# Moving the row-norm scaling between GpSimd and VectorE in an attention and mixer kernel on Trainium2: squares, scales and transposes of the second and third batch reordered

## The chip, the cores and the metric

The kernel runs on one core of one Trainium2 chip. The metric is the device time of one execution in microseconds. Five engines work side by side: TensorE (PE in the profile) for matmuls, VectorE (DVE), ScalarE (ACT), GpSimd (POOL) and SyncE (SP), which here only issues transfers.

## The reference

Cosine attention over 8 batches of 12 heads, 448 rows and head size 64, and a channel mixer behind it:

```python
q_n = q / (np.linalg.norm(q, axis=-1, keepdims=True) + 1e-06)
k_n = k / (np.linalg.norm(k, axis=-1, keepdims=True) + 1e-06)
scores = np.matmul(q_n, k_n.transpose(0, 1, 3, 2)) / tau
scores = scores - np.max(scores, axis=-1, keepdims=True)
attn = np.exp(scores)
attn = attn / (np.sum(attn, axis=-1, keepdims=True) + 1e-09)
out = np.matmul(attn, v)
...
x = np.ascontiguousarray(attn_out.transpose(0, 2, 1, 3)).reshape(B, S, H * D)
...
xt = x.transpose(0, 2, 1)
h = xt @ U @ V
u = x + h.transpose(0, 2, 1)
ch = np.maximum(u @ w_ch1, 0.0) @ w_ch2
return (u + ch).astype(np.float32)
```

x is 8 x 448 x 768, U is 448 x 32, w_ch1 is 768 x 3072, w_ch2 is 3072 x 768. Everything is given and returned in float32.

## The kernel before

**Tiling.** The 12 heads of a batch are 6 pairs, and the 48 pairs are numbered through: pair 6 is the first of the second batch (b = 1), pair 12 the first of the third. A row of 448 positions is cut into four chunks of up to 128. Loading and preparation go by groups of pairs: groups 0 to 3 are the first batch (of 1, 1, 2 and 2 pairs), and from then on every group has two pairs: group 4 is pairs 6 and 7, group 5 pairs 8 and 9, group 6 pairs 10 and 11, group 7 pairs 12 and 13, group 8 pairs 14 and 15. The loads of q, k and v go to three sets of buffers in turn (`qst`, `kst`, `vst`), the scaled q and k to two (`qk`).

**Preparation of a group** (class `Prep`). `square` (L234) multiplies q or k by itself on GpSimd; `reduce` (L239, VectorE) sums the squares of a row; `root` (L244, L245, ScalarE) takes the square root as Ln and Exp; `invert` (L251, L253, VectorE) makes the inverse; `scale` (L259, on the engine that is given) multiplies q or k of one pair by it and writes bf16. `values` (L267, GpSimd) casts v.

**A pair.** T transposes scaled q and k, into `qkT`: below pair 12 as eight PE matmuls (L288) with an eviction by VectorE (L293), from pair 12 on as one DMA transpose that SP issues (L303). Sc makes the scores (`sc`, L312 and L318) and ScalarE their exponentials (`E`, L326 and L329). V is the product with v in two halves (`av` or `up`, L349 and L356), and VectorE divides by the row sums into X (L367, L368). A (L389) and the following transpose of X (L403) and H (L414) add the low-rank part; VectorE or ScalarE then evicts into `uE` or `uO` (L419). `A` of a pair reads X of both its halves. From pair 12 on variants with DMA transposes (XT, A2, H2) do the same.

**The mixer of a batch** is cut in pieces that are handed out among the pairs of the next batch (the list `fill`; `f(n)` takes the next n). `steps_m1` has 24 pieces, six matmuls each into `mp` (L483), with a relu on ScalarE (L487) or VectorE (L489), whichever a running estimate finds free first (`est.act_first`). `steps_m2` has 24 (first batch) or 32 pieces of six matmuls (L510); after four of them a block of 128 x 384 is complete, goes to `o_sb` (L524, L526, L528), and SP stores it in two halves (`t4`, L534; `t3` or `t4e`, L537 and L540). In the first batch three matmuls with the identity (L520) add u.

**Order.** Every engine runs its instructions in the order in which the program names them; nothing is rescheduled. The first six pairs follow a list written by hand (`ORDER`), at whose end stand the scales of pair 6, `sc6q.v sc6k.v`, both on VectorE. Then a loop goes over pairs 6 to 48: for each pair an `order` of steps, between which `spread` gives out pieces of the mixer by weight. `put(n, i, ...)` hangs a step of preparation behind step i of pair n. SP's queue holds the loads, the DMA transposes and the stores, all in program order; GpSimd's own queue holds the loads of the mixer's weights (`load_w1`, `load_w2`).

Before the change the squares of a group are one step (k, then q), GpSimd scales k and VectorE q, and a line in front of the loop reads:

```python
    preps[4].values()
    preps[4].scale(1, 1, P_)
    preps[4].scale(0, 1, V_)
    fill.extend(steps_m1(0) + steps_m2(0))
    f(3)
    T(NP)
    f(1)
```

Here NP is 6, `V_` is VectorE and `P_` is GpSimd; scale's first argument is 0 for q and 1 for k, the second the pair in the group.

Of the kernel before, what the change touches and what calls it, by code (L numbers as in the profile page):

```python
# [22 lines left out]
def kernel(  # L23
# [16 lines left out]
    nc = tc.nc  # L40

    B, H, S, D = q.shape
# [3 lines left out]
    NP = H // 2  # L46
# [37 lines left out]
    est = Estimate()  # L84
# [85 lines left out]
    groups = []  # L170
# [101 lines left out]
    def by_dma(n):  # L272

        return n >= 2 * NP
# [57 lines left out]
    def step_S(b, p, cs):  # L332
        for c in cs:
            pe_S(b, p, c)
            exp_S(b, p, c)
# [47 lines left out]
    def u_of(b):  # L383
        return uE if b % 2 == 0 else uO
# [83 lines left out]
    def turn(b, half):  # L468
# [4 lines left out]
            out=t.rearrange("p k c d -> p (k c) d"),  # L473
            in_=u_of(b)[:, 3 * half:3 * half + 3, :].rearrange("p k s -> p (k s)"))

    def steps_m1(b):
        u = u_of(b)
        o = 64 if b % 2 == 0 else 0

        def one(f):  # L480
            mp = psum.tile([128, S], FP, name="mp", tag="ps_m", bufs=2)
            for cc in range(CC):
                nc.tensor.matmul(out=mp, lhsT=w1_sb[:, cc, f * 128:(f + 1) * 128],  # L483
                                 rhs=u[:, cc, 0:S], start=(cc == 0), stop=(cc == CC - 1))
            est.pe(1.13)
            if est.act_first(0.55, 0.62):
                nc.scalar.activation(out=relu[:, f, o:o + S], in_=mp, func=AF.Relu)  # L487
            else:
                nc.vector.tensor_scalar_max(out=relu[:, f, o:o + S], in0=mp, scalar1=0.0)  # L489
            if b > 0 and f in (3, 12):  # L490
                turn(b, f // 12)

        return [lambda f=f: one(f) for f in range(NC)]

    def steps_m2(b):
        u = u_of(b)
        if b % 2 == 0:
            chunks = [(64 + 128 * c, 128 * c, c) for c in range(3)]
        else:
            chunks = [(384, 384, 3)] + [(128 * c, 128 * c, c) for c in range(3)]  # L500
        steps = []
        state = {}

        def part(half, ci, lo, hi):
            r0, u0, c = chunks[ci]
            if lo == 0:
                state["mp"] = psum.tile([128, HC], FP, name="mp", tag="ps_m", bufs=2)
            mp = state["mp"]
            for f in range(lo, hi):
                nc.tensor.matmul(out=mp, lhsT=relu[:, f, r0:r0 + 128],  # L510
                                 rhs=w2_sb[:, f, half * HC:(half + 1) * HC],
                                 start=(f == 0), stop=(b > 0 and f == NC - 1), skip_group_check=True)
            est.pe(0.97)
            if hi < NC:
                return
            o = work.tile([128, HC], FP, name="o_sb", tag="o_sb", bufs=3)
            if b == 0:
                for i in range(3):
                    cc = half * 3 + i
                    nc.tensor.matmul(out=mp[:, i * 128:(i + 1) * 128], lhsT=u[:, cc, u0:u0 + 128],  # L520
                                     rhs=ident, start=False, stop=(i == 2), skip_group_check=True)
                est.pe(0.17)
                if est.act_first(0.48, 0.55):
                    nc.scalar.copy(out=o, in_=mp)  # L524
                else:
                    nc.vector.tensor_copy(out=o, in_=mp)  # L526
            else:
                nc.vector.tensor_add(o.rearrange("p (k d) -> p k d", d=128),  # L528
                                     mp.rearrange("p (k d) -> p k d", d=128),
                                     ut_of[(b, half)][:, :, c, :])  # L530
                est.dve(0.55)
            cols = slice(half * HC, (half + 1) * HC)
            t4 = out[b, 0:256, cols].rearrange("(p c) d -> c p d", c=4)
            nc.sync.dma_start(out=t4[c], in_=o[0:64, :])  # L534
            if c < 3:
                t3 = out[b, 256:448, cols].rearrange("(p c) d -> c p d", c=3)
                nc.sync.dma_start(out=t3[c], in_=o[64:128, :])  # L537
            else:
                t4e = out[b - 1, 0:256, cols].rearrange("(p c) d -> c p d", c=4)
                nc.sync.dma_start(out=t4e[3], in_=o[64:128, :])  # L540

        for half in range(2):
            for ci in range(len(chunks)):
                for i in range(4):
                    steps.append(lambda half=half, ci=ci, i=i: part(half, ci, 6 * i, 6 * i + 6))
        return steps
# [4 lines left out]
    fill = []  # L551
    preps = [Prep(gi) for gi in range(len(groups))]
    first_pair = [b * NP + p0 for b, p0, _ in groups]

    def f(n):
        for _ in range(n):
            fill.pop(0)()
# [16 lines left out]
    V_, P_ = nc.vector, nc.gpsimd  # L574

    def T(n):
        step_T(*pairs[n])

    def Sc(n, *cs):
        step_S(*pairs[n], cs)  # L580

    def V(n, half):
        step_V(*pairs[n], half)

    def A(n):
        step_A(*pairs[n])

    def Hs(n):
        step_H(*pairs[n])
# [77 lines left out]
    load_w2(0, 0, 12)  # L667
    load_w2(0, 12, 24)
    preps[4].values()
    preps[4].scale(1, 1, P_)  # L670
    preps[4].scale(0, 1, V_)
    fill.extend(steps_m1(0) + steps_m2(0))
    f(3)
    T(NP)
    f(1)


# [2 lines left out]
    def put(n, at, fn):  # L680
        after.setdefault((n, at), []).append(fn)

    for gi in range(5, len(groups)):
        m, n, g = first_pair[gi], groups[gi][2], preps[gi]
        two = range(n)
        if m - 3 < NP:
            at = [(NP, 0), (NP, 6), (NP, 5), (NP, 6), (NP + 1, 0), (NP + 1, 1), (NP + 1, 2), (NP + 1, 3)]
        elif m == 2 * NP:
            at = [(m - 2, i) for i in (0, 6, 3, 4, 5)] + [(m - 1, i) for i in (0, 1, 2)]
        elif m - 3 == NP + 1:  # L690
            at = [(NP + 1, 6), (NP + 2, 5)] + [(NP + 2, i) for i in (3, 4, 5, 6)] + [(NP + 3, 0), (NP + 3, 2)]
        else:
            at = [(m - 3, 0), (m - 3, 5)] + [(m - 2, i) for i in range(6)]
        put(*at[0], lambda g=g: (g.square(1), g.square(0)))
        put(*at[1], lambda g=g: g.values())
        put(*at[2], lambda g=g: g.reduce(1))
        put(*at[3], lambda g=g: g.reduce(0))
        put(*at[4], lambda g=g: g.root())
        put(*at[5], lambda g=g: (g.invert(), [g.scale(1, j, P_) for j in two]))
        for j in two:  # L700
            put(*at[6 + j], lambda g=g, j=j: g.scale(0, j, V_))
        if gi > 5 and m - 6 <= NP:
            put(*((NP, 3), (NP + 3, 0))[gi - 6], lambda gi=gi: load_all(gi))
        elif gi > 5:
            put(m - 6, 4, lambda gi=gi: load(gi, "q", nc.sync))
            put(m - 5, 5, lambda gi=gi: load(gi, "k", nc.sync))
            put(m - 4, 3, lambda gi=gi: load(gi, "v", nc.sync))
        if by_dma(m):
            put(m - 1, -1 if m > 2 * NP else 2, lambda m=m: T(m))
            put(m - 1, 0 if m > 2 * NP else 4, lambda m=m: T(m + 1))  # L710
# [21 lines left out]
    for n in range(NP, NPAIR + 1):  # L732
        b, p = pairs[n] if n < NPAIR else (B, 0)
# [2 lines left out]
        late = n > FIRST2  # L736
        for g in after.pop((n, -1), []):
            g()
        if not late:
            if n % 2 == 0:  # L740

                order = [
                    (1, lambda: Sc(n, 0, 1)),
                    (0, done and (lambda: V(n - 1, 0))),
                    (1, not by_dma(n + 1) and (lambda: T(n + 1))),
                    (0, lambda: Sc(n, 3)),
                    (1, done and (lambda: V(n - 1, 1))),
                    (0, done and (lambda: A(n - 1))),
                    (1, lambda: (Sc(n, 2), Sc(n + 1, 0))),
                    (1, done and (lambda: Hs(n - 1))),  # L750
                ]
            else:
                order = [
                    (1, lambda: Sc(n, 1, 2)),
                    (1, lambda: V(n - 1, 0)),
                    (0, lambda: Sc(n, 3)),
                    (1, not by_dma(n + 1) and (lambda: T(n + 1))),
                    (1, lambda: V(n - 1, 1)),
                    (1, lambda: A(n - 1)),
                    (0, lambda: Hs(n - 1)),  # L760
                ]
            last = p == 0 and done
            nf = len(fill) if last else 5
            spread(n, order, nf)
            if last:
                f(len(fill))
                fill.extend(steps_m1(b - 1) + steps_m2(b - 1))
            continue
# [80 lines left out]
```

## Time and profile before

| what | value |
|---|---|
| time, median of 3 runs | 596.05 us (595.59 to 596.13) |
| profiled run | 595.31 us, span in the trace 593.5 us |
| PE busy | 574.4 us (97%) |
| VectorE busy | 258.7 us (44%) |
| ScalarE busy | 263.6 us (44%) |
| GpSimd busy | 190.1 us (32%) |
| granted PE clock, mean | 0.995 |
| HBM read, written | 52.19 MB, 11.01 MB |

A profile is one execution. Its span starts with the first instruction; times in the text count from there. A line of a group or of the timeline names the engine, the line of the kernel, the operation, and the tile that is written and those that are read (out<-in); the idle time in brackets is what the engine stood before it, with the instruction that ended the wait. An idle engine costs time only where the work that ends last runs through it. The span is some 2 us shorter than the time of the same run.

### The profile page before, as it was taken

The page shows a single profiled execution, that of the slowest core. Times are in us where ns is not written, and L with a number is a line of the kernel's source. Part 1 is how long each engine was busy: PE and PEld are TensorE (multiplying, and loading weights), DVE is VectorE, ACT ScalarE, POOL GpSimd, SP SyncE. Part 2 cuts the span into 40 slices and gives each one's busy share as a digit, 9 for nine tenths or more (in the row PEclk, how much of TensorE's full clock was granted, in tenths as well). Part 3 has the DMA queues.
Part 4 walks back from the last instruction along what each step waited for, and adds up shares of the span by engine and source line. Part 5 has one row for each costly group of instructions (what it writes and reads, how often), then busy time and mean ns, then how long its engine had stood idle before and what let it go on. Part 6 is the DMA issues. An engine that isn't in the chain of part 4 may idle for free.

```text
span 593.5 us, 11562 instructions
## 1 busy us (share of the span) xinstructions
PE 574.4 (97%) x4729; PEld 327.7 (55%) x4729; DVE 258.7 (44%) x499; ACT 263.6 (44%) x452; POOL 190.1 (32%) x161
## 2 busy tenths in 40 slices
PE   6988997999999999999999999999999999999996
PEld 5654564554555555655555555555556545555564
DVE  6875665516345255633354263643355242220011
ACT  5965453446434465246343465345542465314300
POOL 8674555504054053143152251351340410000000
PEclk9999998999999999999999999999999999999999
DMA  6999999463474763673655753863646631222012
GB/s 165 204 230 233 241 240 196 112 117 82 112 152 114 155 134 93 141 170 85 127 135 112 160 129 86 159 158 76 140 110 138 134 64 28 51 64 47 6 48 54
DMA packets 138581, 74.20 MB, mean 125 GB/s; under 512 B 85568, under 2 KB 138352, under 8 KB 138528
## 3 DMA queue, kind: packets, MB, share of 16 engines
q1 hardware_dynamic: 128496, 63.06, 46.9%
q0 software_dynamic: 9728, 10.18, 10.1%
q8 instruction: 37, 0.61, 0.4%
q10 hardware_dynamic: 304, 0.21, 0.1%
q14 instruction: 16, 0.13, 0.1%
HBM read 52.19 MB, written 11.01 MB: 106 GB/s over the span
## 4 chain that ended last, share of the span: by engine, by line
PE 90%; DVE 3%; DMA 3%; SPq 1%; ACT 1%; POOL 1%; issue 1%; POOLq 0%; DVEq 0%; ACTq 0%
PE mp L510 37%; PE mp L483 35%; PE sc L318 5%; PE av L356 3%; DMA kst<-in_k_dram 2%; PE up L356 2%; PE sc L312 1%; DVE qk L259 1%; PE av L349 1%; PE up L349 1%; PE up L442 1%; PE tp L288 1%; DMA qst<-in_q_dram 1%; POOL sq L234 1%; PE av L455 1%
## 5 line engine op out<-in xcount | busy, mean ns | idle before, releaser
L510 PE MATMUL mp<-w_sb,relu 128*128 128x384 bf16 x1344 | 237.2, 328 | 0.0
L510 PEld LDWEIGHTS <-relu 128*128 128x128 bf16 x1344 | 126.0, 98 | 92.4 <-issue 15.8
L483 PEld LDWEIGHTS <-w_sb 128*128 128x128 bf16 x1152 | 107.3, 98 | 101.1 <-issue 10.2
L329 ACT ACTIVATE E<-sc 128x896 bf16<-128x896 f32 x144 | 124.5, 916 | 67.2 <-PE sc L318 66.6
L487 ACT ACTIVATE relu<-mp 128x448 bf16<-128x448 f32 x166 | 90.3, 544 | 138.0 <-PE mp L483 137.9
L259 POOL TENSOR_TENSOR qk<-kst,inv 128x512 bf16<-128x512 f32 x44 | 53.0, 1223 | 264.0 <-DVE inv L253 257.0
L483 PE MATMUL mp<-uE,w_sb 128*128 128x448 bf16 x576 | 119.3, 353 | 0.8 <-DVE relu L489 0.8
L483 PE MATMUL mp<-uO,w_sb 128*128 128x448 bf16 x576 | 115.6, 353 | 0.0
L528 DVE TENSOR_TENSOR o_sb<-mp,ut 128x384 f32<-128x384 f32 x50 | 27.8, 556 | 122.6 <-PE mp L510 122.6
L239 DVE TENSOR_REDUCE ss<-sq 128x16 f32<-128x1024 f32 (+1 forms) x50 | 56.8, 1165 | 4.1 <-POOL sq L234 2.9
L259 DVE TENSOR_TENSOR qk<-qst,inv 128x512 bf16<-128x512 f32 x44 | 51.7, 1183 | 0.6 <-DVE inv L253 0.2
L367 DVE RECIPROCAL rd<-av 128x4 f32<-128x4 f32 x54 | 9.7, 179 | 91.8 <-PE av L356 91.8
L234 POOL TENSOR_TENSOR sq<-kst 128x1024 f32<-128x1024 f32 (+1 forms) x23 | 44.4, 1932 | 14.6 <-DMA kst<-in_k_dram 14.6
L356 PEld LDWEIGHTS <-E 128*128 128x128 bf16 x1152 | 45.0, 97 | 0.0
L234 POOL TENSOR_TENSOR sq<-qst 128x1024 f32<-128x1024 f32 x21 | 43.3, 2061 | 0.0
L318 PE MATMUL sc<-qkT 64*128 64x448 bf16 x288 | 41.3, 355 | 0.9 <-ACT E L326 0.3
L326 ACT ACTIVATE E<-sc 128x448 bf16<-128x448 f32 x48 | 25.9, 540 | 32.4 <-PE sc L312 32.4
L267 POOL CAST v<-vst 128x1024 bf16<-128x1024 f32 (+1 forms) x25 | 28.4, 1138 | 9.5 <-DMA vst<-in_v_dram 6.9
L356 PE MATMUL av<-v,E 128*128 128x65 bf16 x648 | 29.1, 193 | 0.0
L489 DVE TENSOR_SCALAR relu<-mp 128x448 bf16<-128x448 f32 x26 | 16.0, 620 | 29.7 <-PE mp L483 29.3
L349 PEld LDWEIGHTS <-E 128*128 128x128 bf16 x192 | 17.9, 98 | 16.2 <-DVE uO L460 0.8
L367 DVE RECIPROCAL rd<-up 128x4 f32<-128x4 f32 x36 | 6.5, 181 | 44.9 <-PE up L356 44.9
(93 smaller groups left out, 321.9 us busy)
## 6 DMA issues: line engine op xcount, KB each, us to landing
out_dram<-o_sb SPq DMA_DIRECT2D x112, 96.0 KB, 2.2
w_sb<-in_moe_w_ch_dram POOLq DMA_DIRECT2D x8, 1152.0 KB, 25.8
qst<-in_q_dram SPq DMA_DIRECT2D x23, 256.0 KB, 4.0
vst<-in_v_dram SPq DMA_DIRECT2D x46, 128.0 KB, 2.8
kst<-in_k_dram SPq DMA_DIRECT2D x44, 128.0 KB, 2.7
qst<-in_q_dram SPq DMA_DIRECT2D x23, 192.0 KB, 4.0
vst<-in_v_dram SPq DMA_DIRECT2D x46, 96.0 KB, 2.6
kst<-in_k_dram SPq DMA_DIRECT2D x44, 96.0 KB, 2.7
```

Source lines behind the costliest of these rows:

```text
L234: nc.gpsimd.tensor_mul(sq[:, 0:self.nh * 4, :], self.flat(t), self.flat(t))
L239: nc.vector.reduce_sum(self.ss[:, j, 0:self.nh * 4], self.sq[j][:, 0:self.nh * 4, :], axis=AX.X)
L259: eng.tensor_mul(qks[self.gi % 2][:, j, i, :, :, :], t[:, 2 * j:2 * j + 2, :, :].rearrange("p h c d -> p c h d"), iv.unsqueeze(3).to_broad ...
L267: nc.gpsimd.tensor_copy(out=self.flat(v65[self.s])[:, :, 0:D], in_=self.flat(vst[self.s]))
L318: nc.tensor.matmul(out=sc[:, h, 0:S], lhsT=t[r, 1, c * 128:(c + 1) * 128], rhs=t[r, 0, 0:S], start=True, stop=True)
L329: nc.scalar.activation(out=e[:, 2 * c:2 * c + 2, 0:S], in_=sc[:, :, 0:S], func=AF.Exp)
L349: nc.tensor.matmul(out=av[:, i, :, :], lhsT=e[:, 6, ic * 128:(ic + 1) * 128], rhs=vv[:, 2 * j:2 * j + 2, 3, :], start=(i == 0), stop=False ...
L356: nc.tensor.matmul(out=av[:, i, h, :], lhsT=e[:, 2 * c + h, ic * 128:(ic + 1) * 128], rhs=vv[:, 2 * j + h, c, :], start=False, stop=(i == ...
L483: nc.tensor.matmul(out=mp, lhsT=w1_sb[:, cc, f * 128:(f + 1) * 128], rhs=u[:, cc, 0:S], start=(cc == 0), stop=(cc == CC - 1))
L487: nc.scalar.activation(out=relu[:, f, o:o + S], in_=mp, func=AF.Relu)
L510: nc.tensor.matmul(out=mp, lhsT=relu[:, f, r0:r0 + 128], rhs=w2_sb[:, f, half * HC:(half + 1) * HC], start=(f == 0), stop=(b > 0 and f == ...
L528: nc.vector.tensor_add(o.rearrange("p (k d) -> p k d", d=128), mp.rearrange("p (k d) -> p k d", d=128), ut_of[(b, half)][:, :, c, :])
```

## The change

It does four things. In preparation, q and k of a group are squared in steps of their own, with places of their own, and so are the scales: for group 5 (pairs 8 and 9) VectorE scales both k and q; for group 7 (pairs 12 and 13) GpSimd scales both; the other groups keep k on GpSimd and q on VectorE, and k of pair 7 moves to VectorE. Where a group's sums are taken, the order of q and k may turn: in group 6 VectorE now sums q before k. The transpose of pair 6 comes after five pieces of the mixer and not three, and before the scales of pair 7; the transposes of pairs 8 and 10 come after the second half of V of the pair before. During pair 7 all relus go to ScalarE (`busy`). And for the second half of the columns of the last batch three stores (`t3`) are issued by ScalarE and not by SP. In even pairs a transpose that is left to DMA now counts in the weights of `spread`, which moves mixer pieces in pair 12.

```diff
+    state_of = {"busy": False}
...
-            if est.act_first(0.55, 0.62):
+            if state_of["busy"] or est.act_first(0.55, 0.62):
...
-                nc.sync.dma_start(out=t3[c], in_=o[64:128, :])
+                other = nc.scalar if b == B - 1 and half == 1 else nc.sync
+                other.dma_start(out=t3[c], in_=o[64:128, :])
...
-    preps[4].scale(1, 1, P_)
+    fill.extend(steps_m1(0) + steps_m2(0))
+    f(5)
+    T(NP)
     preps[4].scale(0, 1, V_)
-    fill.extend(steps_m1(0) + steps_m2(0))
-    f(3)
-    T(NP)
+    preps[4].scale(1, 1, V_)
     f(1)
...
+        scales = [(1, 0, P_), (1, 1, P_), (0, 0, V_), (0, 1, V_)]
+        if m == NP + 2:
+            at = [(NP, 0), (NP, 1), (NP + 1, 6), (NP, 5), (NP + 1, 0), (NP + 1, 1)]
+            when = [(NP + 1, 2), (NP + 1, 5), (NP + 1, 2), (NP + 1, 5)]
+            scales = [(1, 0, V_), (1, 1, V_), (0, 0, V_), (0, 1, V_)]
+        elif m == NP + 4:
+            at = [(NP + 2, 0), (NP + 2, 0), (NP + 2, 6), (NP + 2, 3), (NP + 2, 4), (NP + 2, 5)]
+            when = [(NP + 2, 6), (NP + 2, 6), (NP + 3, 0), (NP + 3, 2)]
         elif m == 2 * NP:
-            at = [(m - 2, i) for i in (0, 6, 3, 4, 5)] + [(m - 1, i) for i in (0, 1, 2)]
+            at = [(m - 2, 0), (m - 2, 0), (m - 2, 6), (m - 2, 4), (m - 2, 3), (m - 2, 5)]
+            when = [(m - 1, 0)] * 4
+            scales = [(1, 0, P_), (0, 0, P_), (1, 1, P_), (0, 1, P_)]
         else:
-            at = [(m - 3, 0), (m - 3, 5)] + [(m - 2, i) for i in range(6)]
+            d = 1 if m == 2 * NP + 2 else 0
+            at = [(m - 3, 0), (m - 3, 0), (m - 3, 5)] + [(m - 2, i + d) for i in (1, 0, 2)]
+            when = [(m - 2, i + d) for i in (3, 3, 4, 5)]
+        put(*at[1], lambda g=g: g.square(1))
+        put(*at[0], lambda g=g: g.square(0))
+        put(*at[2], lambda g=g: g.values())
+        put(*at[4], lambda g=g: g.reduce(1))
         put(*at[3], lambda g=g: g.reduce(0))
+        put(*at[5], lambda g=g: g.root())
+        put(*when[0], lambda g=g: g.invert())
+        for x, w in zip(scales, when):
+            put(*w, lambda g=g, x=x: g.scale(*x))
...
+        state_of["busy"] = n == NP + 1
...
-                    (1, not by_dma(n + 1) and (lambda: T(n + 1))),
+                    (1, None if by_dma(n + 1) else (lambda: T(n + 1))),
...
+                    (1, lambda: V(n - 1, 1)),
                     (1, not by_dma(n + 1) and (lambda: T(n + 1))),
-                    (1, lambda: V(n - 1, 1)),
```

## The prediction

> **What bounds the kernel now.** I read the busy time by stage first, then who TensorE (PE) waited for, then the timelines around each wait. By stage (columns: window, its length, busy us and instruction count of PE, weight loads, VectorE, ScalarE, GpSimd, then granted PE clock, DMA share, GB/s):
>
> ```profile
> 39.30:62.00 22.70, 18.40 (x125) 9.09 (x124) 14.24 (x22) 11.27 (x20) 13.46 (x11) 1.00 1.16 235
> 62.00:85.00 23.00, 23.00 (x220) 13.35 (x219) 12.96 (x25) 13.52 (x25) 12.95 (x11) 1.00 1.23 240
> 85.00:99.00 14.00, 11.69 (x128) 7.47 (x125) 10.54 (x15) 6.06 (x11) 6.85 (x6) 1.00 1.16 227
> 99.00:124.00 25.00, 23.73 (x175) 13.94 (x175) 8.95 (x17) 8.22 (x15) 9.82 (x9) 0.93 0.43 104
> 124.00:560.00 436.00, 435.92 (x3452) 242.08 (x3450) 177.29 (x340) 195.90 (x337) 116.66 (x77) 1.00 0.50 111
> ```
>
> From 124 to 560 us PE is busy 435.92 of 436.00: it sets the time there, and nothing but fewer PE instructions could shorten it. What can be won lies before 124 us: idle PE and one stretch at a clock of 0.93. PE's waits in 40 to 125 us (us in total, times, longest):
>
> ```profile
> PE av L389 <- DVE X L368: 3.0, 1, 3.0
> PE tp L288 <- DVE qk L259: 1.8, 2, 1.7
> PE tp L288 <- POOL qk L259: 1.4, 1, 1.4
> PE mp L483 <- DVE relu L489: 0.8, 1, 0.8
> PE av L349 <- DVE X L368: 0.5, 1, 0.5
> PE sc L318 <- ACT E L326: 0.3, 1, 0.3
> ```
>
> The largest, in the timeline of PE, then of VectorE, then of GpSimd (start, length, operation, idle before):
>
> ```profile
> 99.72 0.48 PE L389 MATMUL av<-X,U_sb 128*128 128x128 bf16 x4 [3.04 <-DVE X L368]
> 100.38 3.54 PE L510 MATMUL mp<-w_sb,relu 128*128 128x384 bf16 x12
> 94.48 4.63 DVE L259 TENSOR_TENSOR qk<-qst,inv 128x512 bf16<-128x512 f32 x2
> 99.24 0.42 DVE L368 TENSOR_TENSOR X<-av,rd 128x256 bf16<-128x256 f32 x1
> 94.37 1.89 POOL L234 TENSOR_TENSOR sq<-kst 128x1024 f32<-128x1024 f32 x1
> 96.22 2.34 POOL L234 TENSOR_TENSOR sq<-qst 128x1024 f32<-128x1024 f32 x1
> ```
>
> The two q scales of pairs 12 and 13 take 4.63 us where the shortest row of that kind takes 0.68, because GpSimd squares the next group meanwhile. X of pair 10 stands behind them, and A of pair 10 waits 3.04. Then twelve m2 matmuls take 3.54 us instead of 2.06 to 2.12: the clock record shows 0.5 from 99.87 for 3.41 us.
>
> **What the skill says.** The Trainium skill, "GPSIMD Engine Reference", section 1 (Specifications): GpSimd's SBUF interface is shared with VectorE, in contention with VectorE instructions that have two SBUF inputs. The trace agrees: 0.68 alone, 1.3 to 1.5 beside GpSimd's scales, 2.3 beside its squares. "TensorE: Matmul & The Clock Gate", Part 1: the clock falls to half after an idle window of about 3.4 us and returns after a busy one. Here 3.04 us of idling did it, 1.66 did not. "DMA: Bandwidth & Descriptors", "Queues, rings and completion order": an engine's descriptors are consumed in ring order; SP's transfers landed in issue order up to 100 us here.
>
> **The change, part by part.** PE's order is the same from the end of pair 12 to the end of the kernel, so only 40 to 122 us and the last store can change. A modelled matmul end lies 0.16 after the next start, so idle of x costs x + 0.16. One m1 part (six L483 matmuls) is 1.13 us, one m2 part 0.97.
>
> 1. T(6) after five m1 parts, not three. VectorE's first two scales end at about 43.7 with GpSimd idle (44.56 before); PE comes at 39.30 + 5 x 1.13 + 0.09 = 45.07. The 1.66 idle (1.82 lost) goes.
>
> 2. Both scales of pair 7 move to VectorE behind T(6)'s eviction (46.35) while GpSimd squares q, landed at 46.11, until 48.16. One scale contended (to 48.3), one alone: 49.0. T(7) would be ready at 48.28: new wait 0.75 (0 without contention, 1.3 with both contended).
>
> 3. With two relus moved, the wait of m1 for VectorE (0.78, 0.94 lost) goes; a relu now stands before exp on ScalarE: Sc(7,0) waits 0.24 more.
>
> 4. Pair 8's scales are all on VectorE with GpSimd idle (its next input lands at 65.2): four of 0.68. T(8), moved behind V(6,1), waits 0.25 instead of 1.38 and 0.15. Sc(8) thus starts at about 64.3 with two m1 parts more done, against 65.62.
>
> 5. Here the gain shrinks. k of pairs 10 and 11 lands at 65.20 as before, since SP's order is unchanged up to there. GpSimd squares k, then q:
>
> ```profile
> 65.36 1.89 POOL L234 TENSOR_TENSOR sq<-kst 128x1024 f32<-128x1024 f32 x1 [3.72 <-DMA kst<-in_k_dram]
> 67.21 1.89 POOL L234 TENSOR_TENSOR sq<-qst 128x1024 f32<-128x1024 f32 x1
> ```
>
> VectorE now reduces q first: it stands at 69.15 until the later square, reduces until 70.28, and only then makes X(7,1), at 70.9. A(7), ready at 69.85, starts at 70.95: 1.1 us of waiting, which also swallows errors in 2 to 4. Before it started at 71.15 with two m1 parts fewer. Kept: 0.20 + 2.27 = 2.47.
>
> 6. Pair 9 to 11 follow at PE's pace; at Sc(10) two m2 parts take the place of two m1: 0.52 + 1.95 = 2.47 again. In pair 11 no q scale is on VectorE, so X(10,1) is there at 95.6 and A(10) does not wait. The chain from Sc(10) at 82.7, by the durations above, reaches Sc(12) at 98.65 with two m2 parts and their three identity matmuls more (2.12); before, 104.04. Gain 5.39 + 2.12 = 7.5, of which about 5 are the idle and the half clock. With m2 parts now between V(11,0) and V(11,1), the wait of 0.55 (0.71 lost) goes: 8.2.
>
> 7. The price: T(12) is a DMA transpose on SP's queue. GpSimd's four scales start at about 91.4, 1.04 each (its row beside k scales), so T(12) can be issued at 94.6 instead of 96.95. But the store of the first m2 block is now made early, and stands in SP's order before the v and q loads of later groups: it waits for ScalarE's copy at 87.0, and those loads, issued at 81.5 to 86 before, come at 88 to 92. In front of T(12) lie two stores' worth of 192 KB each and loads of 448 + 448 KB: 1,280 KB, 1.31 MB. In 88 to 93 us SP's queue moved 0.63 MB in 5 us (the w2 loads take the rest), so from about 88.3 they take 10.4: to 98.7. A transpose landed 2.66 after its forerunner (97.45 to 100.11), or some 1.8 after it if its packets follow at once: 100.5 to 101.4, I take 101.0. Sc(12), ready at 98.65, waits 2.35. Bounds: 0 if the loads are short of that, 3.2 with another 0.8 us of queue. T(13) is not needed until some 9 us later.
>
> 8. Three last t3 stores go from SP to ScalarE's queue. Only the last counts: SP issues t4 at 589.65 and t3 at 590.16, landed at 592.37. In parallel t3 lands like t4, at 591.74 to 592: 0.5 saved (0.3 to 0.6; a loss only if the two issues block each other, against which SP's and ScalarE's first issues, at 0.75 and 0.78, overlapped).
>
> Moved loads, squares and reductions of groups after pair 12 lie under PE work (VectorE is free some 60% of the time there).
>
> Sum: 8.2 - 2.35 + 0.5 = 6.35 against this profile's span of 593.5, which belongs to a run of 595.31; taken from the median, 596.05 - 6.35 = 589.7.
>
> **Rivals.** (a) T(12) is not late: the w2 loads end sooner and leave SP's queue the whole rate. For it: SP's share rose once w2 was done. Then 596.05 - 8.7 = 587.35. (b) The wait at Sc(12) reaches 3.2 and halves the clock again, as at 99.87, another 1.7 (3.41 x 0.5): 8.7 - 3.2 - 1.7 = 3.8 gained, 592.25. (c) Slower: SP's queue in front of T(12) moves at half the rate, 63 KB per us, as small packets beside w2 and late stores might make it. It ends at 109.1, T(12) lands at 111.4, Sc(12) waits 12.75 and the clock costs 1.7: 596.05 - 8.7 + 14.45 = 601.8. It decides once T(12) lands later than 98.65 + 7.0 = 105.65, at a rate below some 87 KB per us; the lowest that I see beside the w2 loads while SP's queue is full is about 107. (d) No change: VectorE, with more scales, delays X everywhere in pairs 6 to 9; against it, A(7) is pinned by a landing and not by them.
>
> **Chances.** Main case 0.62, (a) 0.16, (b) 0.16, (c) 0.04, (d) 0.02. Range 587.2 to 592.6: it takes in (a) and (b). A measurement of this kernel tells about 0.2%, 1.2 us, from no change: faster 0.94, same 0.02, slower 0.04.
>
> **What would show it.** After: no PE wait at L288 before T(6); A(7) waiting some 1.1 us for VectorE's X; no 3.0 wait at A(10) and no half clock near 100; q scales of pairs 12, 13 on GpSimd; a PE wait of about 2.3 us for the transposed qkT at Sc(12), near 98.7; m1 of batch 1 starting at about 116.8 (122.61 before). A(7) without a wait, Sc(12) without one or with a half clock after it, or idle PE after 124 us, would prove a step wrong.

## The result, and the profile after

The changed kernel takes 589.3 us (median, 589.16 to 589.77) against 596.09 for the kernel before in the same comparison: a ratio of 0.9881, interval 0.9856 to 0.9905. The forecast of 589.7 was right, and so were most of its steps. Two errors inside it were not small, but one landing made them cancel, and that landing was itself met partly by luck.

By stage, in the columns of the prediction's first view:

```profile
39.30:62.00 22.70, 21.72 (x158) 11.46 (x157) 14.67 (x24) 12.94 (x24) 10.03 (x8) 1.00 1.16 236
62.00:85.00 23.00, 20.51 (x180) 11.57 (x177) 11.35 (x23) 10.79 (x20) 12.38 (x11) 0.93 1.23 240
85.00:99.00 14.00, 14.00 (x153) 9.01 (x152) 7.38 (x16) 7.51 (x13) 5.74 (x6) 1.00 1.14 236
99.00:124.00 25.00, 25.00 (x208) 14.94 (x207) 11.09 (x19) 9.82 (x18) 12.56 (x11) 1.00 0.61 134
124.00:560.00 436.00, 435.92 (x3433) 242.12 (x3432) 175.39 (x336) 193.56 (x332) 116.86 (x77) 1.00 0.50 109
```

The last stage is as full as before, 435.92 us: nothing there moved. In the first, third and fourth, 6.90 of the 7.88 us of idle PE are gone (4.30, 2.31 and 1.27 before; 0.98, 0 and 0 now). The second stage was full before and now holds both an idle of 2.49 us and the clock of 0.93, which stood in the fourth. All that PE waits for between 40 and 125 us is three lines:

```profile
PE av L389 <- DVE X L368: 2.5, 1, 2.5
PE sc L318 <- ACT E L326: 0.6, 1, 0.6
PE tp L288 <- DVE qk L259: 0.4, 1, 0.4
```

The wait of L389 has the name of the largest one before (3.0), but is another: it was A of pair 10 near 99 us, and is A of pair 7 near 71. No wait for a transposed qkT is there. The timeline of PE around A(7) and at Sc(12):

```profile
71.87 0.58 PE L389 MATMUL av<-X,U_sb 128*128 128x128 bf16 x4 [2.49 <-DVE X L368]
...
73.62 2.12 PE L485 MATMUL mp<-uE,w_sb 128*128 128x448 bf16 x6
...
100.95 0.35 PE L414 MATMUL up<-V_sb,A_sb 128*128 128x448 bf16 x1
101.28 0.55 PE L318 MATMUL sc<-qkT 64*128 64x448 bf16 x4
```

Six m1 matmuls take 2.12 us at 73.62 where others take 1.30: the clock record shows 0.5 from 71.89 for 3.41 us. VectorE, then GpSimd, show why A(7) waits:

```profile
70.05 1.22 DVE L239 TENSOR_REDUCE ss<-sq 128x16 f32<-128x1024 f32 x1 [2.76 <-POOL sq L234]
71.19 0.17 DVE L367 RECIPROCAL rd<-av 128x4 f32<-128x4 f32 x1
71.39 0.42 DVE L368 TENSOR_TENSOR X<-av,rd 128x256 bf16<-128x256 f32 x1
```

```profile
66.28 1.89 POOL L234 TENSOR_TENSOR sq<-kst 128x1024 f32<-128x1024 f32 x1 [6.40 <-DVE rd L367]
68.13 1.88 POOL L234 TENSOR_TENSOR sq<-qst 128x1024 f32<-128x1024 f32 x1
...
93.95 1.06 POOL L259 TENSOR_TENSOR qk<-kst,inv 128x512 bf16<-128x512 f32 x1 [8.26 <-DVE inv L253]
94.97 1.06 POOL L259 TENSOR_TENSOR qk<-qst,inv 128x512 bf16<-128x512 f32 x1
```

The sum of q stands before X(7,1) in VectorE's order and idles 2.76 us for the later square. (The square of k is put down to VectorE's rd, but its last load landed at 66.11, 0.17 before; in other runs of this order the profile names that load.) The scales of pairs 12 and 13 are on GpSimd, 1.06 each. T(12) in SP's order, where each line is an issue and the last one holds the transposes of pairs 12 and 13:

```profile
89.44 0.54 SPq L536 DMA_DIRECT2D out_dram<-o_sb  x1
...
95.07 0.61 SPq L198 DMA_DIRECT2D qst<-in_q_dram  x1
96.06 0.52 SPq L536 DMA_DIRECT2D out_dram<-o_sb  x1
96.62 0.60 SPq L540 DMA_DIRECT2D out_dram<-o_sb  x1
97.33 2.75 SPq L303 DMA_TRANSPOSE qkT<-qk  x2
```

It stands behind the early store, the loads and a second store. It landed at 101.23, and Sc(12) starts at 101.28. PE's own work before it ends at the same moment, so no idle time of PE is booked; but the load of the weights for Sc(12), which PE must have first, was released by the landing (its gap of 0.28 us is hardly more than usual, so the two ends coincide):

```profile
101.27 0.11 PEld L318 LDWEIGHTS <-qkT 64*128 64x128 bf16 x4 [0.28 <-DMA qkT<-qk]
```

### The profile page after: what moved, and what is told of

The parts are those of the page before. It is cut to its first block, busy times and chain, and to the rows that moved or that the text cites. A ratio compares the mean times of both kernels' runs of the same rounds, so it can differ in the third digit from the quotient of the medians.

```text
span 587.6 us, 11561 instructions
## 1 busy us (share of the span) xinstructions
PE 574.8 (98%) x4729; PEld 328.9 (56%) x4729; DVE 254.3 (43%) x500; ACT 263.6 (45%) x452; POOL 187.8 (32%) x160
## 4 chain that ended last, share of the span: by engine, by line
PE 89%; DMA 6%; DVE 1%; SPq 1%; ACT 1%; issue 0%; DVEq 0%; ACTq 0%; POOLq 0%
PE mp L512 38%; PE mp L485 34%; PE sc L318 5%; PE av L356 3%; DMA qst<-in_q_dram 3%; PE up L356 2%; DMA kst<-in_k_dram 2%; PE sc L312 1%; DMA vst<-in_v_dram 1%; PE av L349 1%; PE up L349 1%; PE up L442 1%; PE av L455 1%; PE tp L288 1%; ACT E L329 0%
## 5 line engine op out<-in xcount | busy, mean ns | idle before, releaser
L259 POOL TENSOR_TENSOR qk<-kst,inv 128x512 bf16<-128x512 f32 x41 | 49.6, 1226 | 259.5 <-DVE inv L253 259.5
L259 DVE TENSOR_TENSOR qk<-qst,inv 128x512 bf16<-128x512 f32 x42 | 45.7, 1094 | 0.5
```

What stands on the lines that cost most here:

```text
L259: eng.tensor_mul(qks[self.gi % 2][:, j, i, :, :, :], t[:, 2 * j:2 * j + 2, :, :].rearrange("p h c d -> p c h d"), iv.unsqueeze(3).to_broad ...
```

## The experiments

Each ratio is to the kernel before, timed on the same chip; kernels of different sets are best compared by it. The changed kernel has two measurements: 0.9881 (above) and 0.9902 (the last of this section). Spans and waits belong to the profiled execution alone. In the expectations L is the theory that the landing of T(12) sets Sc(12), and P the rival that PE's own work before it does.

**Take one of two waits in a row away.** In the changed kernel group 6 sums k first, so that A(7) need not wait for the later square.

```
-            at = [(NP + 2, 0), (NP + 2, 0), (NP + 2, 6), (NP + 2, 3), (NP + 2, 4), (NP + 2, 5)]
+            at = [(NP + 2, 0), (NP + 2, 0), (NP + 2, 6), (NP + 2, 4), (NP + 2, 3), (NP + 2, 5)]
```

> The changed kernel, but in group 6 VectorE sums k before q again. Theory P (what is left to win is PE's wait at A(7), 2.49 us, and the half clock behind it): X(7,1) comes at about 69.9, the wait falls to some 0.7 and the clock stays at 1.0, so 1.9 + 1.7 = 3.6 are gained: 585.7. Theory L (Sc(12) starts when the DMA transpose T(12) has landed, and that is set by the bytes ahead of it, near 100.5 to 101.2 whatever PE does before): Sc(12) waits some 3.5 us, the clock is halved there, and the time is 588.6 to 590.5.

Measured: 591.29 us, ratio 0.9941 (0.992 to 0.9962), some 2 us slower than the changed kernel. The timeline of PE:

```profile
97.72 0.35 PE L414 MATMUL up<-V_sb,A_sb 128*128 128x448 bf16 x1
100.84 0.69 PE L318 MATMUL sc<-qkT 64*128 64x448 bf16 x4 [2.77 <-DMA qkT<-qk]
101.46 3.06 PE L512 MATMUL mp<-w_sb,relu 128*128 128x384 bf16 x9
```

A(7) no longer waits and PE is at Sc(12) by 98, but T(12), now issued at 94.10, lands at 100.79. The wait has moved and nothing is won; the half clock that follows it (0.5 from 101.12) lies after the landing, where nothing absorbs it: 1.7 us more. P, which wanted 585.7, is false. L has the order of events, but not all of the sizes: the wait was 2.8 and not 3.5, and the time lies above its 588.6 to 590.5.

**Free the queue in front of T(12), with A(7) waiting and without.** The q load of group 9 goes behind T(13); the second kernel sums k first too.

```
-            put(m - 6, 4, lambda gi=gi: load(gi, "q", nc.sync))
+            put(*((m - 5, 6) if m == 2 * NP + 4 else (m - 6, 4)), lambda gi=gi: load(gi, "q", nc.sync))
```

> The changed kernel, but SP issues the q loads of group 9 (448 KB) behind T(13) and not ahead of T(12). Theories P and L both expect no gain, 589.3, since PE reaches Sc(12) at 101.1 by itself; but L expects T(12) to land some 2 us earlier, near 99, and if it still lands after 100.7 the bytes ahead of it are not what sets its landing.

> Both edits: k summed before q in group 6, and q of group 9 loaded behind T(13). Theory P: 585.7, as with the first edit alone. Theory L: Sc(12) ready at about 97.3, T(12) landed at 98 to 98.5, so about 1 us of waiting without a half clock: 586.5, and the first edit alone is at least 2 us slower than this.

Measured: 588.33 us, 0.9898 (0.9877 to 0.992), and 588.11 us, 0.9889 (0.987 to 0.9907). T(12) landed at 100.10 and 100.12, only 1.1 earlier than in the changed kernel, and in the second only 0.7 earlier than with k first alone. PE's waits in the second:

```profile
PE sc L318 <- DMA qkT<-qk: 1.8, 1, 1.8
PE av L389 <- DVE X L368: 0.9, 1, 0.9
```

In the second the wait has again gone from A(7) to Sc(12). In the first A(7) waited 2.18, without a half clock, and PE came to Sc(12) by its own work at 100.15, within 0.1 of the landing. So both start Sc(12) alike, at 100.15 and 100.17, and taking A(7)'s wait away paid nothing. Both expectations of L missed in size: it had T(12) near 99 and at 98 to 98.5, and 586.5 for the second. What 448 KB in front of T(12) cost was over-rated.

**Take more out of the queue.** k first, the q loads of group 9 and also the v loads of group 8 behind T(13).

```
-            put(m - 4, 3, lambda gi=gi: load(gi, "v", nc.sync))
+            put(*((m - 3, 4) if m == 2 * NP + 2 else (m - 4, 3)), lambda gi=gi: load(gi, "v", nc.sync))
```

> The changed kernel, k summed first in group 6, and both the v loads of group 8 and the q loads of group 9 (896 KB) issued behind T(13), so that only the two stores stand ahead of T(12). Ring theory (the bytes ahead of it on SP's queue set T(12)'s landing): it lands by 98, Sc(12) hardly waits, 586.0 to 586.5. Weights theory (SP's packets are held back until the last weight load on GpSimd's queue is through, near 97 to 98.5): it still lands at 99.5 or later, Sc(12) waits 1.3 to 2 us, 587.5 to 588.3.

Measured: 586.96 us (585.49 to 589.55), 0.986 (0.9837 to 0.9882). SP's issues:

```profile
91.71 0.47 SPq L536 DMA_DIRECT2D out_dram<-o_sb  x1
92.22 0.60 SPq L540 DMA_DIRECT2D out_dram<-o_sb  x1
92.93 3.31 SPq L303 DMA_TRANSPOSE qkT<-qk  x2
```

T(12) landed at 97.31, 3.9 earlier, and Sc(12) waited 0.4. So what stands ahead of it makes the landing late, as the prediction said; the w2 loads alone do not (the weights theory wanted 99.5 or later). The time is just above the 586.0 to 586.5 of the ring theory, with a wide spread. The w2 loads count too, since the two queues share the DMA engines: from 88 to 93 us they moved 1.03 MB in the changed kernel, where SP's queue moved nothing, and 0.57 MB beside SP's 0.63 in the kernel before. An estimate from the 236 GB/s of all queues in 85 to 99 us: 896 KB less is worth 3.9 us, and 3.5 (against k first alone) to 3.9 were found; 448 KB is 1.9, where 0.7 to 1.1 were found. Why the first half brought less stays open.

**Take T(12) off the queue.** Pair 12 is transposed by PE (eight matmuls, 0.61 us, and VectorE's eviction), with k summed first; then the same without k first.

```
-        if not by_dma(b * NP + p):
+        if b * NP + p <= 2 * NP:
...
-            put(m - 1, -1 if m > 2 * NP else 2, lambda m=m: T(m))
+            if m > 2 * NP:
+                put(m - 1, -1, lambda m=m: T(m))
...
-                    (1, not by_dma(n + 1) and (lambda: T(n + 1))),
+                    (1, n < 2 * NP and (lambda: T(n + 1))),
```

> The changed kernel, k summed before q in group 6, and pair 12 transposed on PE (eight matmuls, 0.45 us, with VectorE's eviction) and not by DMA. Theory L (PE's gain at A(7) was taken back because T(12) landed at 100.1 to 101.2 in every kernel so far): the wait at Sc(12) goes, so against the run with k first alone 2.9 + 1.7 - 0.45 = 4.1 are gained: a ratio to the kernel before near 0.987, 586.5 to 587.5. Rival W (what holds Sc(12) is not the transfer; another wait, for GpSimd's scales of pair 12 or for the last w2 load, takes its place): no faster than 588.5.

> The changed kernel with pair 12 transposed on PE alone. PE reached Sc(12) at 101.1 by itself with T(12) landed at 101.2, so theory L expects nothing to gain and 0.45 us to pay: 589.3 to 589.8, with the wait at A(7) still there. Were it faster by 1 us or more, the landing and not A(7) would have been the limit of the changed kernel.

Measured: 586.26 us (586.03 to 586.94), 0.9848 (0.9828 to 0.9869), and 588.59 us (587.68 to 590.43), 0.9892 (0.987 to 0.9915). PE in the first:

```profile
97.53 0.35 PE L414 MATMUL up<-V_sb,A_sb 128*128 128x448 bf16 x1
97.81 0.55 PE L318 MATMUL sc<-qkT 64*128 64x448 bf16 x4
```

Sc(12) starts 3.47 us earlier than in the changed kernel, m1 of the next batch 3.46 earlier (113.48 for 116.94), and the span is 3.4 shorter (584.2). With the landing out of the way the same edit that cost 2 us above pays: what held its Sc(12) was the landing of T(12), and rival W, which wanted 588.5 or more, is false. The second kernel keeps a wait at A(7), 1.10 in its profile, and its ratio lies between the two of the changed kernel: no difference. The first has the lowest median of all; its five times lie below every time of the changed kernel, though its interval overlaps that of the changed kernel's first measurement. From the one with the late v loads it can't be told apart.

**Engine or place of group 7's q scales.** Three kernels: the kernel before with those two on GpSimd and nothing else; the kernel before with them left on VectorE but right behind the inverse; the changed kernel with them back on VectorE, in that same place.

```
-        put(*at[5], lambda g=g: (g.invert(), [g.scale(1, j, P_) for j in two]))
+        if m == 2 * NP:
+            put(*at[5], lambda g=g: (g.invert(), [g.scale(i, j, P_) for j in two for i in (1, 0)]))
+            two = ()
...
```

```
-            put(*at[6 + j], lambda g=g, j=j: g.scale(0, j, V_))
+            put(*(at[5] if m == 2 * NP else at[6 + j]), lambda g=g, j=j: g.scale(0, j, V_))
```

```
-            scales = [(1, 0, P_), (0, 0, P_), (1, 1, P_), (0, 1, P_)]
+            scales = [(1, 0, P_), (1, 1, P_), (0, 0, V_), (0, 1, V_)]
```

> The kernel before with one part of the change alone: GpSimd scales q of pairs 12 and 13 as well as k. The wait at A(10), 3.04 us, and the half clock behind it, 1.7 to 1.85, go: 596.1 - 4.9 = 591.2 if Sc(12) need not wait. Theory L adds a wait at Sc(12), ready at 99.1, for T(12), which could land at 99.5 to 100: 591.6 to 592.1. A rival, that the squares of group 8 (now behind four scales) come too late for VectorE: 593 or more.

> The kernel before with one edit: VectorE keeps q of pairs 12 and 13, but scales it straight after the inverse, ahead of X of pair 10, and so beside GpSimd's k scales and not beside its squares. Place theory (the 4.63 us came from meeting the squares, so the place is enough and the engine does not matter): the two take 2.2 to 3, A(10) waits no longer, the same as with q on GpSimd, 592.2 or a ratio of 0.9957. Engine theory (VectorE must be rid of them): A(10) still waits 2 us or more, 594.5 to 595.5.

> The changed kernel with q of pairs 12 and 13 scaled on VectorE again, k on GpSimd. The port theory: VectorE's two scales, beside GpSimd's scales and squares, take 3 to 4.6 us instead of 1.4, X of pair 10 stands behind them, PE waits 2 to 3 us near 97 and T(12) is issued later: 591.5 to 593. The rival, that the gain of the change came from its first part alone: 589.5.

Measured: 592.24 us, 0.9957 (0.9941 to 0.9974); 592.27 us, 0.9946 (0.9928 to 0.9963); 590.09 us, 0.9915 (0.9895 to 0.9934). In the first two the wait of A(10) and the half clock behind it are gone alike. The first lies just above L's 591.6 to 592.1, and the second came out as its place theory had it. VectorE, then GpSimd, in the second:

```profile
93.45 2.16 DVE L259 TENSOR_TENSOR qk<-qst,inv 128x512 bf16<-128x512 f32 x2
95.53 0.17 DVE L367 RECIPROCAL rd<-av 128x4 f32<-128x4 f32 x1
95.73 0.42 DVE L368 TENSOR_TENSOR X<-av,rd 128x256 bf16<-128x256 f32 x1
```

```profile
93.49 3.02 POOL L259 TENSOR_TENSOR qk<-kst,inv 128x512 bf16<-128x512 f32 x2 [6.68 <-DMA qst<-in_q_dram]
96.48 1.89 POOL L234 TENSOR_TENSOR sq<-kst 128x1024 f32<-128x1024 f32 x1
```

Two scales on VectorE take 2.16 us beside GpSimd's scales, where they took 4.63 beside its squares, and X follows at 95.73. Taking them off VectorE removes A(10)'s wait, but so does another place in VectorE's order: what cost the 3 us was that they met the squares. The third kernel missed its expectation (it was to be slowed by contention on VectorE, to 591.5 or more): its two scales took 2.16 us there too, and X of pair 10 was not late. Its PE waited 1.6 at A(7) and 1.6 at Sc(12), for a T(12) that landed at 101.78.

> The fastest kernel so far (k summed first in group 6, pair 12 transposed on PE) with q of pairs 12 and 13 on VectorE right after the inverse. Place theory: no difference, 586.3, ratio 0.985. Engine theory: X of pair 10 is late, 588 or more.

This is the fastest kernel with those q scales back on VectorE. Measured: 587.28 us (586.51 to 589.21), 0.9867 (0.9845 to 0.9888): the intervals of the two overlap, so engine and place are again not told apart by time, and the profile has no wait at A(10). Its wait at A(7), 1.83 though k is summed first, comes from k of group 6, which landed only at 67.17 in that execution.

**The front part alone.** In the kernel before, T(6) after five pieces and both scales of pair 7 behind it on VectorE; nothing else.

```
-    preps[4].scale(1, 1, P_)
-    preps[4].scale(0, 1, V_)
...
-    f(3)
+    f(5)
     T(NP)
+    preps[4].scale(0, 1, V_)
+    preps[4].scale(1, 1, V_)
```

> The kernel before with the first part of the change alone: five pieces of m1 before T(6), both scales of pair 7 on VectorE after it. The wait of 1.66 us at T(6) goes (1.82), perhaps also m1's wait for a relu (0.94); the rest stays, with the half clock near 100: 593.3 to 594.3. If gains before pair 12 were wholly taken back by T(12)'s landing, as rival, 595.5 or more; but in the kernel before Sc(12) starts at 104.04, 3.9 us after the landing, so theory L expects them kept.

Measured: 595.54 us (592.37 to 599.84), 0.9995 (0.9976 to 1.0015). A miss. T(6) does not wait, but VectorE, then PE, show a new wait:

```profile
54.84 1.22 DVE L239 TENSOR_REDUCE ss<-sq 128x16 f32<-128x1024 f32 x1 [4.64 <-POOL sq L234]
56.69 1.22 DVE L239 TENSOR_REDUCE ss<-sq 128x16 f32<-128x1024 f32 x1 [0.63 <-POOL sq L234]
57.82 0.61 DVE L489 TENSOR_SCALAR relu<-mp 128x448 bf16<-128x448 f32 x1
```

```profile
55.39 0.55 PE L318 MATMUL sc<-qkT 64*128 64x448 bf16 x4
58.49 1.30 PE L483 MATMUL mp<-uE,w_sb 128*128 128x448 bf16 x6 [2.55 <-DVE relu L489]
```

PE comes to a relu that stands on VectorE behind sums of squares, and k of that group landed no earlier (GpSimd's square of it began at 52.92, before at 51.79). The 1.66 us taken from one wait come back as 2.55 and a half clock, and the wait of A(10) with its own half clock is there as before. In the changed kernel no such wait for a relu comes; there the squares have steps of their own and the relus of pair 7 go to ScalarE. Which of the two keeps it away was not tried.

**The changed kernel once more**, as it is.

> The changed kernel as it is, as the measure for the three others of this set on the same chip: 589.3, a ratio near 0.988.

Measured: 589.61 us (588.6 to 590.93), 0.9902 (0.9881 to 0.9922). A(7) waited 2.3 us, the half clock came at 72.64, T(12) landed at 101.50 and Sc(12) waited 0.5. The order of events is that of the first profile; the sizes move by some tenths. Three of the six executions had no half clock at all (granted clock 1.000): 588.60, 589.46 and 589.79, against 589.54, 589.68 and 590.93 for the other three. So the half clock behind A(7), 1.7 us of PE's work, hardly shows in these six times, as it should be where a landing sets Sc(12).

## Why the prediction was right

The forecast was 6.35 us less on the span; the profiled spans differ by 5.9 (593.5 and 587.6). By its steps:

1. *T(6)*: its wait of 1.66 is gone, as predicted.
2. *T(7)*: 0.75 of new waiting was predicted, none came. q landed later than in the profile of before, GpSimd's square began only at 47.06, and the two scales took 0.68 and 0.69 at 45.95 and 46.55. It is the lower bound of the step; it changes nothing behind A(7), which waits for a landing.
3. *Relus*: the wait for VectorE went; Sc(7,0) waits 0.58 instead of 0.34, the 0.24 that was predicted.
4. *T(8)*: 0.40 of idle for 0.25.
5. *A(7)*: the mechanism was right and the size was off. A(7) started at 71.87 instead of 70.95, since k of group 6 landed at 66.11 and not at 65.20; the prediction had taken one execution's landing as fixed. In the 14 profiles it lies between 65.17 and 67.17, and late also in two kernels without this front part (66.02 and 66.40), so the change is not what delays it. Where it came at 65.47 (T(12) on PE alone), A(7) waited the 1.10 that was predicted, and PE came to Sc(12) at 99.47 with the transpose's matmuls in its chain, near the predicted 98.65. As PE also came earlier than foreseen, the wait was 2.49 and not 1.1. It halved the clock, which the prediction had not priced here: 3.41 x 0.5 = 1.7 us.
6. *A(10)*: the wait and its half clock are gone, as is V(11,1)'s. The step named the engine; the kernels above show that another place in VectorE's order would have been enough.
7. *T(12)*: landed at 101.23, predicted 101.0, but not in the way of the step. It was issued at 97.33 and not at 94.6: the scales began at 93.95, not 91.4, and SP stood at a second store until 96.06. SP's queue was to work from 88.3 to 98.7, at 126 KB per us; in the trace no packet of it starts between 87.93 and 93.26, and then what stood ahead was through at 100.29, at some 186 KB per us, as the w2 loads had run alone before. T(12) landed 0.94 behind that and not 2.3. These three errors, +5.0, -3.4 and -1.4, cancel by luck. The rate of 126 KB per us would also make 896 KB worth 7.3 us, and taking them away brought 3.5 to 3.9. What holds is that the landing hardly follows the issue: with k first T(12) was issued at 94.10 and still landed at 100.79. The wait at Sc(12) of 2.35 did not appear: PE came to it late by 0.92 + 1.7 through step 5, 98.65 + 2.62 = 101.27, and measured is 101.28.
8. *The last store*: before, o_sb was done at 589.63 and the last store landed at 592.37, 2.74 later; now 584.01 and 586.42, 2.41 later. 0.33 saved for 0.5. The issues run side by side:

```profile
584.04 0.47 SPq L536 DMA_DIRECT2D out_dram<-o_sb  x1
584.04 0.50 ACTq L540 DMA_DIRECT2D out_dram<-o_sb  x1
```

The sum closes: m1 of the next batch starts at 116.94 (predicted about 116.8) instead of 122.55 (122.61 in the prediction), 5.61 earlier, and with 0.33 at the end that is 5.9, as the span has it.

So the total was right because Sc(12) starts at the later of two: PE's own chain, and the landing of T(12) near 101. Steps 5 and 7 were wrong by +2.6 and -2.35, and either way Sc(12) starts at about 101. That is shown and not only argued: without A(7)'s wait Sc(12) still started at 100.84; with T(12) off the queue as well it started at 97.81. That PE's own chain ended so near the landing, 101.27 and 101.23, is chance, and by its own sign, an Sc(12) without a wait, the prediction had a step wrong. Of the rivals, (a), T(12) not late, is false by its landing, though its reason, w2 through sooner and SP's queue faster, came true; (b), a wait with a half clock at Sc(12), is what the k-first kernel shows, at 591.29 against the rival's 592.25; (c), SP's queue at half the rate, did not occur; nor did (d), X late through more scales on VectorE: X(7,1) was held by a sum and a landing.

## What to carry to other kernels

Where two waits lie in series and the second is for a transfer whose landing does not depend on the first, don't add or subtract them: the step starts at the later of the two chains, and removing the earlier wait pays nothing until the transfer is sooner. On an in-order engine look at what stands directly in front of the operation that the critical engine waits for; a scale moved from behind GpSimd's squares to beside its scales did as much here as a change of engine, and a sum taken in the order in which its inputs arrive freed A(7). And take a landing from one profile with the spread that executions show, 2 us here.

## What the runs showed of the hardware

**The half clock goes by a fixed grid of windows.** The prediction took the length of an idle as the sign. In these profiles a wait of 1.83 us halved the clock and one of 2.18 did not, so the length alone does not decide. The Trainium skill ("TensorE: Matmul & The Clock Gate", Part 1: The HAM clock gate) says that the activity window is about 3.4 us and free-running. The trace agrees: counted from the first rise of the clock, each fall lies at a whole number of 3.413 us: 28 in the kernel before (4.30 to 99.87), 19 in the changed one (7.04 to 71.89), 16 and 29 in the front-alone kernel. With that grid the idle of PE can be added up window by window:

| kernel | wait of PE, us | most idle in one window, us | half clock next |
|---|---|---|---|
| before, A(10) | 3.04 | 3.04 | yes |
| k first, Sc(12) | 2.77 | 2.77 | yes |
| changed, A(7) | 2.49 | 2.49 | yes |
| front alone, at a relu | 2.55 | 2.19 | yes |
| group 7 early, T(6) | 2.0 | 1.96 | yes |
| fastest with q on VectorE, A(7) | 1.83 | 1.83 | yes |
| before with GpSimd for group 7, relu | 1.87 | 1.93 (with a part of the next wait) | no |
| before, T(6) | 1.66 | 1.66 | no |
| q load late, A(7) | 2.18 | 1.53 | no |

The skill's page puts it as an idle window; here 1.83 of 3.41 us was enough, and up to 1.75 never. Between these, at 1.93, one case goes the other way (ends of matmuls are modelled), so the limit is known only as somewhere near half a window. Where the grid falls against the kernel differs from one execution to the next, so the same wait of some 2 us may or may not cost 1.7 more. A part of the spread of the times goes with it: the mean granted clock is known for every execution, and over 43 of the kernel before the time falls as the clock rises (correlation -0.71), over the 14 of the front-alone kernel too (-0.84; 592.37 us at 1.000, 599.84 at 0.991). It is not all: the kernel with the late v and q loads took from 585.49 to 589.55 at 0.996 to 1.000.

**VectorE's scales and GpSimd's operations take turns.** VectorE's two q scales, then GpSimd's two k scales, one by one, in the kernel before with q scaled right behind the inverse:

```profile
93.45 0.69 DVE L259 TENSOR_TENSOR qk<-qst,inv 128x512 bf16<-128x512 f32 x1
94.06 1.55 DVE L259 TENSOR_TENSOR qk<-qst,inv 128x512 bf16<-128x512 f32 x1
```

```profile
93.49 1.56 POOL L259 TENSOR_TENSOR qk<-kst,inv 128x512 bf16<-128x512 f32 x1 [6.68 <-DMA qst<-in_q_dram]
95.02 1.50 POOL L259 TENSOR_TENSOR qk<-kst,inv 128x512 bf16<-128x512 f32 x1
```

VectorE's first starts 0.04 us ahead of GpSimd's and takes 0.69, as it does alone; GpSimd's takes 1.56, where it takes 1.06 undisturbed. VectorE's second starts behind GpSimd's and ends at 95.60, 0.55 after the end of that one. In the kernel before the same two scales met squares of 1.89 and 2.34 us, and the pair took 4.63. Over the 14 profiles all 323 scales of VectorE that start while a scale, square or cast of GpSimd has more than 0.15 us to go end 0.54 to 0.55 us after it, and all 191 that start shortly ahead of one take 0.68 or 0.69. So a scale that comes second pays what is left of the operation in front of it, up to a whole square, and one that comes first pays nothing; the 1.3 to 1.5 and 2.3 of the prediction are such remainders. The Trainium skill ("GPSIMD Engine Reference", section 1) states the sharing of the interface; these are its sizes here.

**A store that starts late.** The store issued at 89.44 in the changed kernel landed after 5.4 us, where the median of SP's stores is 2.2. The first packet on SP's queue came 3.8 us after its issue (3.8 in the second profile of this kernel, 3.9 with k first), while the w2 load on GpSimd's queue ran. In the kernel before a store issued at 91.28 took 5.5. Why the packets start so late was not tried, and stays open.
